# Attention with a relative bias, then a low-rank mixer and a feed-forward block: opening the first feed-forward tiles on three of four channel blocks, an output tile in pieces, and an earlier weight load

## The chip, the cores and the metric

One core of one Trainium2 chip runs the whole program. The metric is device time in microseconds (us), lower is better, from several executions. A profile is one more execution, recorded by the hardware; its span is a microsecond or two shorter than the time of the same run, as the time also contains the launch.

## The reference, cut to what matters

```python
scores = q @ k.T / sqrt(64)              # 8 batches, 8 heads, 576 positions, 64 wide
attn   = softmax(scores + bias[bucket(i - j)])   # bias: 32 buckets, saturates at |i - j| = 128
x      = (attn @ v)                      # heads side by side: 8 x 576 x 512
u      = x + (x.T @ U @ V).T             # mix over positions, rank 32
out    = u + relu(u @ w1) @ w2           # feed-forward: 512 -> 2048 -> 512
```

## The kernel before

The program works on pairs of heads, four to a batch, 32 in all. For each pair TensorE makes the scores, ScalarE their exponentials (`p_sb`), VectorE multiplies the diagonal band by the exponential of the bias (`eb`), TensorE multiplies by the values (`o`), VectorE normalises into `xp`, and TensorE mixes over positions. The bias table goes out to memory once and comes back as overlapping rows, which GpSimd copies in reverse order into `eb`:

```python
def reverse_eb(pr, copy):
    t = ebr.pop(pr)
    ...
        copy(out=eb[:, 2 * pr : 2 * pr + 2, :],
             in_=_ap_with(t, t.offset + 383, [t.ap[0], [384, 2], [-1, 384]]))
```

All matmuls of the feed-forward block are a stream that is cut into the gaps of the attention. `work.run(us)` places as many matmuls as the budget holds, 0.216 us each, in program order:

```python
def chunk(j, tail):                     # one group of 512 tokens; j = 8 is the remainders
    rhs = uT[j % 3] if j < B else uT_rem
    for nt in range(NHT):               # 16 hidden tiles
        gp_ = acc()                     # a 128 x 512 PSUM tile out of three
        for ct in range(4):             # 4 channel blocks, one per pair of heads
            nc.tensor.matmul(gp_, lhsT=w1b[:, ct, ...], rhs=rhs[:, ct, :], ...)
            yield 0.216
        if (nt % 2) if tail else clock["seg"] > 1.5:
            nc.scalar.activation(g[:, nt, :], gp_, AF.Relu)
        else:
            nc.vector.tensor_relu(out=g[:, nt, :], in_=gp_)
    for tt in range(4):                 # 4 output tiles of 128 tokens
        op = acc()
        for nt in range(NHT):
            nc.tensor.matmul(op, lhsT=g[:, nt, ...], rhs=w2b[:, nt, :], ...)
            yield 0.216
        ...                             # add u on VectorE, store
```

The loads that GpSimd issues while batch 0 runs, in program order:

```python
nc.gpsimd.dma_start(out=gate, in_=gp_dram[0:1, 0:2])   # waits until the table is in memory
load_rem(0, 2)                                         # values of batch 0
for t in range(NKT): load_main(0, 2, t)
reverse_eb(0, nc.gpsimd.tensor_copy)
qk0[3] = [first_qk(which, 3) for which in range(2)]
reverse_eb(1, nc.gpsimd.tensor_copy)
load_w1(0)
load_rem(1, 0); load_rem(1, 1)                         # batch 1
qk1 = [[load_pair(which, 0) for which in range(2)]]
def more_loads():
    for pr in (2, 3): load_eb(pr)
    reverse_eb(2, nc.gpsimd.tensor_copy)
    load_w1(1)
    reverse_eb(3, nc.gpsimd.tensor_copy)
    ...
```

And the main loop, three segments to a pair `g`, from the first pair of batch 1 (`g = 4`) on:

```python
for g in range(NPAIR, NG):
    b, pr = divmod(g, NPAIR)
    for seg in range(3):
        ...                             # scores of this segment
        work.run(1.7 if g < 2 * NPAIR + 2 else 2.2)
        ...                             # mixing, transposes, bands, value matmuls
        if seg and NPAIR < g < 2 * NPAIR:
            put_off.pop(0)()            # an addition of batch 0 that was put off
        ...
        if seg == 1 and b > 1 and pr == 1:
            ready[b - 1] = True         # the next group may start
```

The softmax here doesn't subtract the row's maximum and nothing guards it: scores larger than these inputs give would overflow.

## Time and profile before

| | |
|---|---|
| time, median of 3 | 410.99 us (410.21 to 411.16) |
| TensorE idle around the start of the feed-forward work, 36 to 40 us | 1.49 us |
| eb copy of the last pair of batch 0 ends | 31.29 us |
| value matmuls of that pair start | 34.37 us |
| second group of 512 tokens starts | 94.06 us |

In a timeline a line is: start, duration, engine, source line, operation, output<-inputs, shapes, number merged, and in brackets how long the engine was idle before it and what ended that. TensorE ends are modelled, so waits are best read from the distance of two starts, less the 0.216 us (512 columns), 0.055 us (128) or about 0.03 us (65) of a matmul at full clock.

The TensorE timeline where the first group of tokens has ended and the second begins:

```profile
92.66 0.93 PE L601 MATMUL o<-v_bf,p_sb 128*128 128x65 bf16 x25 [0.95 <-DVE xp L626]
93.52 0.61 PE L514 MATMUL sc<-qkT 64*128 64x512 bf16 x4
94.06 1.25 PE L371 MATMUL acc<-uT,w1b 128*128 128x512 bf16 x5
```

The value matmuls wait 0.95 us for the normalisation of the head before them, because their segment has no feed-forward matmuls to hide it.

### The profile page before, as it was taken

How to read it: one execution, taken by the hardware profiler on the slowest of the kernel's cores; microseconds unless marked ns; L12 is line 12 of the kernel's file. 1: busy time of each engine (PE TensorE's matmuls, PEld its weight loads, DVE VectorE, ACT ScalarE, POOL GpSimd, SP SyncE). 2: the span in 40 equal slices, each digit the busy share in tenths (PEclk: the TensorE clock that was granted, in tenths of full speed). 3: DMA queues.
4: the chain of work that ended last, by engine and by line, in shares of the span. 5: the costliest groups of instructions: out<-in, count | busy, mean ns of one | idle time of the engine just before them, and what ended most of it. 6: DMA issues, size and time to landing. Idle time of an engine off the chain costs nothing.

```text
span 408.5 us, 9084 instructions
## 1 busy us (share of the span) xinstructions
PE 389.5 (95%) x3684; PEld 212.8 (52%) x3684; DVE 246.3 (60%) x558; ACT 205.0 (50%) x284; POOL 125.7 (31%) x179
## 2 busy tenths in 40 slices
PE   3779999999999999999999999999999999999995
PEld 1456555555555555555555555555555554444442
DVE  6886897667765667557754785567656732422421
ACT  5877555556655565556555655556555530220310
POOL 3968924454454045404540454040000000000000
PEclk9799999999999999999999999999999999999999
DMA  7999999999999699949996999399022003001013
GB/s 129 170 170 161 114 189 120 118 118 116 174 69 128 131 117 86 129 104 150 92 102 132 128 89 106 94 138 96 14 66 66 14 14 104 26 14 73 18 27 77
DMA packets 162082, 40.68 MB, mean 100 GB/s; under 512 B 151760, under 2 KB 156888, under 8 KB 162040
## 3 DMA queue, kind: packets, MB, share of 16 engines
q0 software_dynamic: 107904, 17.97, 61.2%
q1 hardware_dynamic: 53320, 21.74, 26.2%
q8 instruction: 29, 0.48, 0.5%
q10 hardware_dynamic: 816, 0.39, 0.4%
q14 instruction: 13, 0.11, 0.1%
HBM read 37.84 MB, written 9.45 MB: 116 GB/s over the span
## 4 chain that ended last, share of the span: by engine, by line
PE 82%; DMA 8%; POOL 6%; DVE 2%; issue 1%; ACT 1%; ACTq 0%; DVEq 0%; POOLq 0%
PE acc L386 31%; PE acc L371 28%; PE o L601 10%; PE sc L514 7%; DMA w1b<-in_moe_w_ch_dram 4%; DMA qb<-in_k_dram 3%; PE acc L637 2%; POOL qb L265 2%; POOL v_bf L255 2%; PE acc L653 1%; PE sc L527 1%; PE sc L548 1%; DMA gp_dram<-gp 1%; DVE ob L396 1%; POOL eb L213 1%
## 5 line engine op out<-in xcount | busy, mean ns | idle before, releaser
L523 ACT ACTIVATE p_sb<-sc 128x1024 bf16<-128x1024 f32 x128 | 124.4, 1022 | 100.4 <-PE sc L514 100.3
L386 PE MATMUL acc<-w2b,g 128*128 128x512 bf16 x576 | 132.4, 379 | 0.0
L371 PE MATMUL acc<-uT,w1b 128*128 128x512 bf16 x512 | 119.5, 380 | 0.6 <-DMA w1b<-in_moe_w_ch_dram 0.4
L371 PEld LDWEIGHTS <-w1b 128*128 128x128 bf16 x576 | 53.2, 98 | 72.4 <-issue 13.1
L386 PEld LDWEIGHTS <-g 128*128 128x128 bf16 x576 | 53.6, 98 | 70.6 <-issue 10.6
L382 DVE TENSOR_SCALAR g<-acc 128x512 bf16<-128x512 f32 x95 | 65.3, 690 | 34.4 <-PE acc L371 33.1
L577 DVE TENSOR_TENSOR p_sb<-p_sb,eb 128x768 bf16<-128x768 bf16 (+3 forms) x160 | 71.3, 472 | 10.0 <-ACT p_sb L523 9.4
L601 PEld LDWEIGHTS <-p_sb 128*128 128x128 bf16 x1600 | 56.1, 98 | 9.2 <-DVE p_sb L577 1.6
L601 PE MATMUL o<-v_bf,p_sb 128*128 128x65 bf16 x1500 | 58.0, 194 | 2.3 <-DVE xp L626 0.9
L380 ACT ACTIVATE g<-acc 128x512 bf16<-128x512 f32 x49 | 29.3, 598 | 59.8 <-PE acc L371 44.5
L396 DVE TENSOR_TENSOR ob<-acc,u_tok 128x512 f32<-128x512 f32 x32 | 22.1, 691 | 49.9 <-PE acc L386 49.9
L514 PE MATMUL sc<-qkT 64*128 64x512 bf16 x256 | 41.3, 392 | 1.5 <-ACT qkT L459 0.7
L905 POOL COPY gate<-xp 1x2 bf16<-1x2 bf16 x18 | 3.5, 197 | 121.5 <-DVE xp L626 121.5
L661 DVE TENSOR_TENSOR u_tok<-acc,xp 128x512 bf16<-128x512 f32 x32 | 22.1, 691 | 23.9 <-PE acc L653 23.7
L626 DVE TENSOR_TENSOR xp<-o,rcp 128x320 bf16<-128x320 f32 x60 | 29.5, 492 | 3.2
L255 POOL DMA_DIRECT2D v_bf<-in_v_dram x32 | 28.4, 911 | 1.7 <-DMA w1b<-in_moe_w_ch_dram 1.4
L255 POOL DMA_DIRECT2D qb<-in_k_dram x24 | 21.7, 906 | 5.8 <-DMA w2b<-in_moe_w_ch_dram 4.2
L255 POOL DMA_DIRECT2D qb<-in_q_dram x24 | 21.9, 913 | 4.7 <-DVE g L382 4.7
L557 ACT ACTIVATE p_sb<-sc 128x640 bf16<-128x640 f32 x32 | 22.3, 698 | 0.2
L540 ACT ACTIVATE p_sb<-sc 128x512 bf16<-128x512 f32 x32 | 19.1, 598 | 5.6 <-PE sc L527 3.9
L624 DVE RECIPROCAL rcp<-o 128x5 f32<-128x5 f32 x60 | 11.5, 191 | 13.7 <-PE o L601 13.2
L645 ACT CAST tt<-acc 128x128 bf16<-128x128 f32 x32 | 8.6, 267 | 14.3 <-PE acc L637 13.8
(90 smaller groups left out, 260.8 us busy)
## 6 DMA issues: line engine op xcount, KB each, us to landing
out_dram<-ob SPq DMA_DIRECT2D x32, 256.0 KB, 2.4
v_bf<-in_v_dram POOLq DMA_DIRECT2D x32, 128.0 KB, 5.9
qb<-in_q_dram POOLq DMA_DIRECT2D x27, 128.0 KB, 4.9
qb<-in_k_dram POOLq DMA_DIRECT2D x27, 128.0 KB, 4.9
w1b<-in_moe_w_ch_dram POOLq DMA_DIRECT2D x2, 1024.0 KB, 8.7
w2b<-in_moe_w_ch_dram POOLq DMA_DIRECT2D x2, 1024.0 KB, 12.6
out_dram<-ob SPq DMA_DIRECT2D x8, 128.0 KB, 2.4
stage<-gp_dram SPq DMA_DIRECT2D x4, 192.0 KB, 4.7
```

The costliest lines, as they stand in the source:

```text
L255: nc.gpsimd.dma_start(out=dst, in_=src[b, :, t * 128 : (t + 1) * 128, :].rearrange("h p d -> p h d"),)
L371: nc.tensor.matmul(gp_, lhsT=w1b[:, ct, nt * 128 : (nt + 1) * 128], rhs=rhs[:, ct, :], start=(ct == 0), stop=(ct == 3),)
L380: nc.scalar.activation(g[:, nt, :], gp_, AF.Relu)
L382: nc.vector.tensor_relu(out=g[:, nt, :], in_=gp_)
L386: nc.tensor.matmul(op, lhsT=g[:, nt, tt * 128 : (tt + 1) * 128], rhs=w2b[:, nt, :], start=(nt == 0), stop=(nt == NHT - 1),)
L396: nc.vector.tensor_tensor(out=ob.rearrange("p (a c) -> p a c", a=NPAIR), in0=op.rearrange("p (a c) -> p a c", a=NPAIR), in1=ur, op=ALU.add,)
L514: nc.tensor.matmul(sp[:, hh, :], lhsT=kT[rows, i * 128 : (i + 1) * 128], rhs=qT[rows, 0:S0], start=True, stop=True,)
L523: nc.scalar.activation(P[:, i, :, 0:S0], sp, AF.Exp, scale=scale)
L557: nc.scalar.activation(P4[:, 0:SP], sp.rearrange("p a c -> p (a c)")[:, 0:SP], AF.Exp, scale=scale,)
L577: nc.vector.tensor_tensor(out=t, in0=t, in1=e, op=ALU.mult)
L601: nc.tensor.matmul(o[:, qt * 66 : qt * 66 + 65], lhsT=lhs[:, c0 : c0 + 128], rhs=rhs, start=(kt == NKT and qt == 0), stop=(kt == NKT - 1), ...
L626: nc.vector.tensor_tensor(out=xo[:, :, hh], in0=o[:, :, 0:64], in1=rbc, op=ALU.mult)
```

## The change

The intent: begin the first three hidden tiles on the channel blocks that exist already, so that TensorE has more to do while the last pair of batch 0 is normalised and mixed; move all of w1 and three value loads earlier in GpSimd's order; and shorten what follows the last matmul by storing the last tile in pieces on two queues. The diff, cut:

```diff
     def chunk(j, tail):
+        ahead = [acc() for _ in range(3)] if j == 0 else []
+        for nt, gp_ in enumerate(ahead):
+            for ct in range(3):
+                first_mm(gp_, rhs, nt, ct)
+                yield 0.216
         for nt in range(NHT):
-            gp_ = acc()
-            for ct in range(4):
+            gp_ = ahead[nt] if nt < len(ahead) else acc()
+            for ct in range(3 if nt < len(ahead) else 0, 4):
 ...
         for tt in range(4):
             op = acc()
+            pieces = (0, 256, 384, 512) if j == B and tt == 3 else (0, 512)
+            for c0, c1 in zip(pieces, pieces[1:]):
+                ...                       # 16 matmuls, addition, store of columns c0:c1
+                        (nc.scalar if par else nc.sync).dma_start(...)   # was nc.sync
 ...
     qk0[2] = [first_qk(which, 2) for which in range(2)]
+    load_rem(0, 2)
+    load_main(0, 2, 0)
 ...
     nc.gpsimd.dma_start(out=gate, in_=gp_dram[0:1, 0:2])
-    load_rem(0, 2)
-    for t in range(NKT):
+    for t in range(1, NKT):
         load_main(0, 2, t)
 ...
     load_w1(0)
-    load_rem(1, 0)
-    load_rem(1, 1)
-    qk1 = [[load_pair(which, 0) for which in range(2)]]
+    load_w1(1)
 ...
         reverse_eb(2, nc.gpsimd.tensor_copy)
-        load_w1(1)
+        load_rem(1, 0)
+        load_rem(1, 1)
+        qk1.append([load_pair(which, 0) for which in range(2)])
         reverse_eb(3, nc.gpsimd.tensor_copy)
 ...
     ready[0] = True
-    work.run(0.64)
-    to_copy[1]()
-    mix_t(3, nc.scalar.copy)
-    mix_ut(3, nc.vector.tensor_copy)
+    work.run(0.215 * 9)
+    sc = [ps_s.tile([128, 2, 512], FP32, name="sc")[:, 0, :] for _ in range(2)]
+    mix_t(3, nc.scalar.copy, sc[0])
+    mix_ut(3, nc.vector.tensor_copy, sc[1])
+    work.run(2.2)
+    for copy in fourth_transposes():      # moved here; was ahead of the last pair's values
+        copy()
+    work.run(1.3)
 ...
-            work.run(1.7 if g < 2 * NPAIR + 2 else 2.2)
+            work.run(1.5 if g < 2 * NPAIR + 2 else 2.2)
 ...
-            if seg and NPAIR < g < 2 * NPAIR:
+            if seg and NPAIR <= g < NPAIR + 3:
                 put_off.pop(0)()
```

More of the change, by code (lines that the diff above doesn't have):

```diff
@@ L296 @@
     held = []
+    qk1 = []
     qk2 = ([], [])
@@ L363, with first_mm @@
     clock = {"seg": 0.0}
+    def first_mm(gp_, rhs, nt, ct):
+        nc.tensor.matmul(
+            gp_,
+            lhsT=w1b[:, ct, nt * 128 : (nt + 1) * 128],
+            rhs=rhs[:, ct, :],
+            start=(ct == 0),
+            stop=(ct == 3),
+        )
     def chunk(j, tail):
@@ L367, in chunk @@
         g = gsb.tile([128, NHT, S0], BF16, name="g")
-        for nt in range(NHT):
-            gp_ = acc()
-            for ct in range(4):
-                nc.tensor.matmul(
-                    gp_,
-                    lhsT=w1b[:, ct, nt * 128 : (nt + 1) * 128],
-                    rhs=rhs[:, ct, :],
-                    start=(ct == 0),
-                    stop=(ct == 3),
-                )
+        ahead = [acc() for _ in range(3)] if j == 0 else []
[3 more added lines that the diff above has]
+                yield 0.216
+        for nt in range(NHT):
+            gp_ = ahead[nt] if nt < len(ahead) else acc()
+            for ct in range(3 if nt < len(ahead) else 0, 4):
+                first_mm(gp_, rhs, nt, ct)
                 yield 0.216
@@ L384, in chunk @@
             op = acc()
-            for nt in range(NHT):
-                nc.tensor.matmul(
-                    op,
-                    lhsT=g[:, nt, tt * 128 : (tt + 1) * 128],
-                    rhs=w2b[:, nt, :],
-                    start=(nt == 0),
-                    stop=(nt == NHT - 1),
-                )
-                yield 0.216
             ob = osb.tile([128, DM], FP32, name="ob")
             ur = u_tok[j % 3][:, :, tt, :] if j < B else u_rem[tt]
-            nc.vector.tensor_tensor(
-                out=ob.rearrange("p (a c) -> p a c", a=NPAIR),
-                in0=op.rearrange("p (a c) -> p a c", a=NPAIR),
-                in1=ur,
-                op=ALU.add,
-            )
-            if j < B:
-                nc.sync.dma_start(out=out[j, tt * 128 : (tt + 1) * 128, :], in_=ob)
-            else:
-                for par in range(2):
-                    nc.sync.dma_start(
-                        out=out[2 * tt + par, S0:S, :],
-                        in_=ob[par * 64 : par * 64 + 64, :],
-                    )
+            pieces = (0, 256, 384, 512) if j == B and tt == 3 else (0, 512)
+            for c0, c1 in zip(pieces, pieces[1:]):
+                w = c1 - c0
+                for nt in range(NHT):
+                    nc.tensor.matmul(
+                        op[:, c0:c1],
+                        lhsT=g[:, nt, tt * 128 : (tt + 1) * 128],
+                        rhs=w2b[:, nt, c0:c1],
+                        start=(nt == 0),
+                        stop=(nt == NHT - 1),
+                        skip_group_check=True,
+                    )
+                    yield 0.216 * w / 512
+                nc.vector.tensor_tensor(
+                    out=ob[:, c0:c1].rearrange("p (a c) -> p a c", c=128),
+                    in0=op[:, c0:c1].rearrange("p (a c) -> p a c", c=128),
+                    in1=ur[:, c0 // 128 : c1 // 128, :],
+                    op=ALU.add,
+                )
+                if j < B:
+                    nc.sync.dma_start(out=out[j, tt * 128 : (tt + 1) * 128, :], in_=ob)
+                else:
+                    for par in range(2):
+                        (nc.scalar if par else nc.sync).dma_start(
+                            out=out[2 * tt + par, S0:S, c0:c1],
+                            in_=ob[par * 64 : par * 64 + 64, c0:c1],
+                        )
     ready = [False] * (B + 1)
@@ L500, in fourth_transposes @@
                 nc.tensor.transpose(tp[:, which, t * 128 : (t + 1) * 128], src, ident)
+        copies = nc.scalar.copy, nc.vector.tensor_copy
         return [
-            lambda w=w: nc.scalar.copy(qkT[1][:, 0, w, :], tp[:, w, 0:SP])
-            for w in range(2)
+            lambda w=w: copies[w](qkT[1][:, 0, w, :], tp[:, w, 0:SP]) for w in range(2)
         ]
@@ L630, with mix_t @@
     tt_pr = {}
-    def mix_t(g, eng):
+    def mix_t(g, eng, tp=None):
         b = g // NPAIR
         x = x_pr[g]
-        tp = acc()
+        tp = acc() if tp is None else tp
         for t in range(NT):
@@ L675, in on_pe, with mix_ut @@
         return g < NPAIR
-    def mix_ut(g, copy):
+    def mix_ut(g, copy, tp=None):
         b, pr = divmod(g, NPAIR)
         x, tt = x_pr[g], tt_pr[g]
-        tp = acc()
+        tp = acc() if tp is None else tp
         nc.tensor.matmul(
@@ L862 @@
     kts(3, 3)
-    to_copy = fourth_transposes()
     bands(3, 4, 0, 1)
     normalise(2)
-    to_copy[0]()
     for kt in (4, 0, 1):
```

## The prediction

> **What bounds the kernel now.** I read the page's busy rows first, then the windows by stage, then the TensorE and GpSimd timelines where TensorE is not full, and the timeline of the last microseconds.
>
> ```profile
> PE   3779999999999999999999999999999999999995
> PEclk9799999999999999999999999999999999999999
> 0.00:18.00 18.00, 9.54 (x75) 4.52 (x75) 13.56 (x56) 12.44 (x17) 11.81 (x21) 0.91 0.98 142
> 18.00:36.00 18.00, 15.16 (x278) 11.68 (x277) 15.58 (x37) 13.54 (x20) 13.95 (x20) 0.90 1.29 174
> 36.00:40.00 4.00, 3.00 (x36) 1.77 (x33) 1.97 (x5) 1.99 (x5) 2.57 (x4) 1.00 2.03 157
> 40.00:95.00 55.00, 53.46 (x577) 30.86 (x577) 42.22 (x95) 29.98 (x40) 30.47 (x44) 1.00 1.37 129
> 95.00:325.00 230.00, 230.00 (x2311) 127.26 (x2310) 148.16 (x326) 132.18 (x182) 66.86 (x94) 1.00 0.98 103
> ```
>
> The first two rows are 40 slices of 10.2 us; the others give stretch, length, then busy time of PE, PEld, VectorE, ScalarE, GpSimd. From 95 to 325 us TensorE has no idle time, so nothing there can be gained without fewer matmul columns, and the change removes none. Idle time lies before 95 us, and after the last matmul. The batch 0 to 1 hand-over:
>
> ```profile
> 20.45 0.43 PE L601 MATMUL o<-v_bf,p_sb 128*128 128x65 bf16 x5 [0.62 <-DMA v_bf<-in_v_dram]
> ...
> 36.60 0.59 PE L371 MATMUL acc<-uT,w1b 128*128 128x512 bf16 x2
> 37.56 0.39 PE L371 MATMUL acc<-uT,w1b 128*128 128x512 bf16 x1 [0.36 <-DMA w1b<-in_moe_w_ch_dram]
> 37.78 0.44 PE L637 MATMUL acc<-xp,upad 128*128 128x128 bf16 x5
> 38.58 0.39 PE L681 MATMUL acc<-vpad,tt 128*128 128x512 bf16 x1 [0.36 <-ACT tt L645]
> ...
> 39.98 1.24 PE L371 MATMUL acc<-uT,w1b 128*128 128x512 bf16 x5 [0.29 <-DVE uT L694]
> ```
>
> Matmul ends are modelled, so I work from starts: back-to-back 512-column matmuls start 0.216 us apart, 128-column ones 0.055. Then the three waits are 0.52, 0.52 and 0.45, 1.49 us together; the value-load wait earlier is 0.84 by the same count. GpSimd in that stage:
>
> ```profile
> 27.90 0.75 POOL L265 DMA_DIRECT2D qb<-in_k_dram  x1 [4.05 <-DMA w1b<-in_moe_w_ch_dram]
> 28.63 0.84 POOL L213 COPY eb<-stage 128x768 bf16<-128x768 bf16 x1
> 29.40 0.70 POOL L347 DMA_DIRECT2D w1b<-in_moe_w_ch_dram  x1
> 30.09 1.20 POOL L213 COPY eb<-stage 128x768 bf16<-128x768 bf16 x1
> ```
>
> Here GpSimd itself stops 4.05 us: the 22nd of its DMAs may not be issued before the 14th, the first half of w1, has landed (27.61), because its completion semaphores go round in eight. The eb copy behind it in program order waits too. The end:
>
> ```profile
> 403.71 0.69 DVE L396 TENSOR_TENSOR ob<-acc,u_rem 128x512 f32<-128x512 f32 x1 [2.76 <-PE acc L386]
> 404.43 1.10 SPq L406 DMA_DIRECT2D out_dram<-ob  x2
> ```
>
> After the last matmul come one addition of 0.69, two output DMAs issued one behind the other (the second at 404.94 lands at 407.32), and 1.1 us of closing.
>
> **The Trainium skill.** "DMA: Bandwidth & Descriptors", section "Issuing engines are not separate DMA queues": issuing from several engines saves only sequencer time. In this trace that time is about 0.5 us for the second of two output DMAs. "TensorE: Matmul & The Clock Gate", section "Back-to-back issue gap", gives 81 ns for a sustained 128-column matmul with its weight load and 131 for 512; this trace has 55 and 216, and I use the trace. "SBUF — State Buffer", section "SBUF: two separate sides", says that a GpSimd operation and a VectorE one with two SBUF inputs exclude each other on a shared port pair; the trace agrees: the band multiply of 256 elements takes 314 ns in the mean but 1.32 us at 28.49, beside the eb copy at 28.63.
>
> **The change, part by part.**
>
> (a) Three value loads go ahead of the wait for the small table. The rest then issue about 2.2 us earlier (two of 0.65, one of 0.9). The wait at 20.45 (0.84, and 0.07 just after) goes; from there to 33 us the engines wait on each other, so the shift carries: -0.9.
>
> (b) The second half of w1 is issued right behind the first. Its own wait at 37.56 is hardly worth anything: that matmul also needs the third channel block of uT, whose ScalarE copy ended at 37.39. But the order of GpSimd's DMAs changes: w1 becomes numbers 14 and 15, the loads of batch 1 numbers 16 to 23, and the copy of eb for the last pair stands behind number 23, which must wait for number 15. Landing of number 15: w1's packets started at 20.8, a half takes about 4.95 (20.8 to 27.0 with its tail, landing 27.61). With the queue about a microsecond earlier, two halves end near 31.0 to 31.5. Then 0.28 wake, 0.75 issue, 0.9 copy: the copy ends near 33.0 (32.3 to 33.8) instead of 31.3. VectorE wants it at about 31 (before 32.2, less (a)). Behind it in order are two bands (1.0) and the first half of a normalisation (0.7) before the value matmuls of the last pair can start: 33.0 + 1.75 = 34.75. Without that stall they would start at 34.37 - 0.9 - 0.5 (ten transposes have moved out) = 33.0. So +1.75.
>
> (c) Opening tiles: nine matmuls on blocks 0 to 2 instead of three, then the last pair's two mixing steps back to back on score buffers, then the last blocks. The third matmul still waits for the uT copy: 0.42. The six more hide the normalisation. The step from tt to its matmul still has nothing between: 0.52. The matmul that follows needs the last uT block at once: VectorE copy 0.69 plus 0.26 of hand-over, 0.95, where before the remainder scores lay in between and 0.45 was left. Three evictions then go to ScalarE one after another, and the fourth tile needs the first one's buffer: 0.2 + 0.6, less 0.43 for two other matmuls, 0.4. Sum 2.3 against 1.49: +0.8. The 23 matmuls more that are placed here (26 for 3) are only moved.
>
> (d) Segments of batch 1 get 1.5 us of feed-forward instead of 1.7 (seven matmuls for eight), and the put-off mixing additions start one pair earlier. From 50 to 80 us start-to-start gaps add to 1.6, nearly all released by VectorE. Six evictions (4.1 us of VectorE) are gone from this stage, but its first two pairs now hold four additions of 0.69 that were in the second and third pair. By count VectorE has 17.5 us of work in those two pairs and TensorE 16.5: about the same loss, then relief. +0.3. The stretch near 91.5 (1.1 us idle, a segment with no feed-forward work, as the next tile group opens at the same place) loses about the same, with one such segment more but less VectorE work: 0.
>
> (e) Last tile in pieces of 256, 128, 128: 16 matmuls each at 0.108, 0.055, 0.055 is 3.49 for 3.46. The last addition shrinks from 0.69 to about 0.28 (a 64x128 one takes 0.285): -0.4. The second DMA no longer waits 0.5 for the first: -0.5. A quarter of the bytes in it: about -0.2. Sum -1.1.
>
> Sum: -0.9 + 1.75 + 0.8 + 0.3 - 1.1 = +0.85, or 411.8. I lower it to 411.0: single waits worked out by hand overlap in part, VectorE's bands run free of the eb copies, and budgets as fine as nine matmuls look tuned against a clock.
>
> **Rivals.** One: the queue of GpSimd does bound the early part, as the page's chain has it:
>
> ```profile
> 18.41 9.20 DMA w1b<-in_moe_w_ch_dram
> ...
> 29.40 8.11 DMA w1b<-in_moe_w_ch_dram
> ```
>
> Then getting w1 in eight microseconds earlier would give several microseconds, and the time would be 405 to 408. Against it: TensorE shows only 1.49 us idle between 36 and 40, one third of it released by w1, and the chain reaches these loads only by way of a 12.3 us load that ends in front of transposes at 63.8 which do not read it. Two: the stall in (b) does not happen, as w1 lands by 29.5 or the copy finds its place; then (a) stands and the sum is near 410. Three: the stall in (b) is longer, as w1 shares the engines with the eb loads, and the transposes then wait for batch 1's loads; 413 to 414. Four: VectorE in (d) is relieved at once, most of the 1.6 us goes, and with rival two it is 408.
>
> **Range and chances.** The idle time before 95 us that can be moved is some 3 to 5 us, and the end gives one; no step adds more than 2 to 3. So 411.0, with 407.5 to 414.0 for eight in ten. Two per cent is 8.2 us, more than all of it: faster 0.03, same 0.94, slower 0.03.
>
> **What would show it.** (a) No wait of a value matmul on v_bf near 20 us. (b) A GpSimd wait of some microseconds on w1b at about 27 to 31, an eb copy ending near 33, a VectorE band released by it and TensorE idle 1 to 2 us before the last pair's value matmuls. (c) Feed-forward matmuls released by uT copies for 0.4 and 0.95. (d) Gaps released by VectorE evictions in the first two pairs of batch 1. (e) Last addition near 0.28, last landing about 2.1 us after its issue. If the eb copy comes before 32, (b) is wrong; if the time is under 407, rival one or four has more in it than I give it.

## The result, and the profile after

The changed kernel took 417.03 us (median of 4, 416.49 to 418.27). The ratio to the kernel before is 1.0155, 95% interval 1.0127 to 1.0183. A ratio here is the mean time of one kernel's runs over the mean of the other's of the same rounds, so it is not quite the ratio of the medians. The change costs 6 us; the prediction was no change, with a range of 407.5 to 414.0. Where medians are subtracted below, it is always from the kernel before as it ran on the same chip (410.4 to 411.0).

Line numbers differ: the first feed-forward layer was L371 and is L367, the second L386 and L400, bands L577 and L590, value matmuls L601 and L614. The kernels of the experiments have their own.

The page's busy row and granted clock of the changed kernel, in 40 slices of 10.4 us, and its window from 33.3 to 40 us:

```profile
PE   3776899997999999999999999999999999999995
PEclk9898999999999999999999999999999999999999
33.30:40.00 6.70, 3.37 (x54) 3.08 (x53) 2.95 (x8) 1.83 (x4) 6.17 (x9) 0.76 1.24 79
```

Three slices have fallen: the fourth (31 to 42 us) from 9 to 6, the fifth, with most of the openings, from 9 to 8, and the tenth (94 to 104 us) from 9 to 7. From 33.3 to 40 us TensorE works 3.37 us of 6.70, and its clock was granted at 0.76 in the mean of this execution.

The first dent, in GpSimd's timeline and the one VectorE line that depends on it:

```profile
24.72 1.55 POOL L265 DMA_DIRECT2D qb<-in_q_dram  x2
28.53 0.75 POOL L265 DMA_DIRECT2D qb<-in_k_dram  x1 [2.26 <-DMA w1b<-in_moe_w_ch_dram]
33.84 0.74 POOL L265 DMA_DIRECT2D qb<-in_k_dram  x1 [4.55 <-DMA w1b<-in_moe_w_ch_dram]
34.57 0.84 POOL L213 COPY eb<-stage 128x768 bf16<-128x768 bf16 x1
...
35.44 0.89 DVE L590 TENSOR_TENSOR p_sb<-p_sb,eb 128x512 bf16<-128x512 bf16 x2 [4.68 <-POOL eb L213]
```

GpSimd stands still twice, 2.26 and 4.55 us, each time in front of a load of batch 1 and each time until a half of w1 has landed (28.25 and 33.55). The eb copy behind the second load in program order has had its input since 22.20, and ends at 35.41 instead of 31.29. VectorE waits 4.68 us for it. Then TensorE:

```profile
37.02 1.01 PE L614 MATMUL o<-v_bf,p_sb 128*128 128x65 bf16 x15 [3.33 <-DVE xp L639]
...
41.55 1.67 PE L367 MATMUL acc<-uT,w1b 128*128 128x512 bf16 x7 [0.24 <-ACT uT L707]
43.06 0.44 PE L650 MATMUL sc<-xp,upad 128*128 128x128 bf16 x5
43.86 0.39 PE L694 MATMUL sc<-vpad,tt 128*128 128x512 bf16 x1 [0.36 <-ACT tt L658]
44.09 0.39 PE L699 MATMUL sc<-ident,xp 128*128 128x128 bf16 x4
45.26 0.81 PE L367 MATMUL acc<-uT,w1b 128*128 128x512 bf16 x3 [0.78 <-DVE uT L707]
46.32 1.02 PE L367 MATMUL acc<-uT,w1b 128*128 128x512 bf16 x4 [0.25 <-ACT g L389]
```

The last pair's value matmuls start at 37.02 instead of 34.37: 2.65 us late, after 3.50 us of idle time by the starts. The four waits at the opening tiles are, by starts, 0.41, 0.52, 0.95 and 0.42, together 2.29 us; a fifth of 0.40, at 50.08, waits for the VectorE copy of the transposes that moved.

The second dent, TensorE at the change of groups, to hold against the three lines of before:

```profile
98.82 0.93 PE L614 MATMUL o<-v_bf,p_sb 128*128 128x65 bf16 x25 [0.69 <-DVE xp L639]
99.67 0.61 PE L527 MATMUL sc<-qkT 64*128 64x512 bf16 x4
100.21 0.82 PE L367 MATMUL acc<-uT,w1b 128*128 128x512 bf16 x3
102.66 1.02 PE L367 MATMUL acc<-uT,w1b 128*128 128x512 bf16 x3 [1.62 <-DMA uT<-u_tok]
```

The wait for the normalisation is still there, and a new one has come: three matmuls of the new group run, and the fourth waits (1.79 us by starts) for the last channel block, a transposing DMA issued at 97.49 that lands at 102.61. Before, the same DMA was issued at 91.33, landed at 93.74, and nothing waited. The end:

```profile
410.61 1.05 PE L400 MATMUL acc<-w2b,g 128*128 128x128 bf16 x16 [0.52 <-DVE ob L409]
411.70 0.29 DVE L409 TENSOR_TENSOR ob<-acc,u_rem 128x128 f32<-128x128 f32 x1 [1.14 <-PE acc L400]
412.05 1.05 PE L400 MATMUL acc<-w2b,g 128*128 128x128 bf16 x16 [0.38 <-DVE ob L409]
413.14 0.29 DVE L409 TENSOR_TENSOR ob<-acc,u_rem 128x128 f32<-128x128 f32 x1 [1.14 <-PE acc L400]
```

The additions have become as short as predicted, but the matmuls of the second and third piece wait for the addition of the piece before. From the start of the addition of the tile before last to the end the kernel before takes 8.24 us and this one 8.11.

### The profile page after: what moved, and what is told of

It is laid out like the page before. It is cut to its first block, busy times and chain, and to the rows that moved or that the text cites. A ratio compares the mean times of both kernels' runs of the same rounds, so it can differ in the third digit from the quotient of the medians. Undisturbed runs are those within 1.5% of the kernel's fastest.

```text
span 416.5 us, 9102 instructions
## 1 busy us (share of the span) xinstructions
PE 387.6 (93%) x3656; PEld 215.4 (52%) x3716; DVE 238.7 (57%) x551; ACT 209.9 (50%) x293; POOL 124.7 (30%) x179
## 4 chain that ended last, share of the span: by engine, by line
PE 84%; DMA 7%; DVE 4%; issue 1%; POOL 1%; ACT 1%; SPq 0%; DVEq 0%
PE acc L400 30%; PE acc L367 29%; PE o L614 10%; PE sc L527 7%; DMA w1b<-in_moe_w_ch_dram 3%; PE acc L650 2%; PE acc L666 2%; PE sc L540 1%; PE sc L561 1%; DMA uT<-u_tok 1%; DMA stage<-gp_dram 1%; DVE p_sb L590 1%; DMA tblT<-in_bias_table_dram 1%; DMA gp_dram<-gp 1%; PE acc L501 1%
## 5 line engine op out<-in xcount | busy, mean ns | idle before, releaser
L400 PE MATMUL acc<-w2b,g 128*128 128x512 bf16 (+2 forms) x580 | 129.6, 368 | 2.6 <-DVE ob L409 0.9
L367 PE MATMUL acc<-uT,w1b 128*128 128x512 bf16 x484 | 115.3, 379 | 4.9 <-DMA uT<-u_tok 1.6
L400 PEld LDWEIGHTS <-g 128*128 128x128 bf16 x608 | 55.5, 98 | 70.9 <-issue 12.6
L367 PEld LDWEIGHTS <-w1b 128*128 128x128 bf16 x576 | 53.4, 98 | 73.8 <-issue 15.7
L391 DVE TENSOR_SCALAR g<-acc 128x512 bf16<-128x512 f32 x85 | 58.3, 690 | 38.5 <-PE acc L367 35.5
L590 DVE TENSOR_TENSOR p_sb<-p_sb,eb 128x768 bf16<-128x768 bf16 (+3 forms) x160 | 70.0, 465 | 15.2 <-ACT p_sb L536 9.9
L389 ACT ACTIVATE g<-acc 128x512 bf16<-128x512 f32 x59 | 35.0, 598 | 62.6 <-PE acc L367 62.2
L614 PEld LDWEIGHTS <-p_sb 128*128 128x128 bf16 x1600 | 56.7, 99 | 12.0 <-DVE xp L639 4.5
L614 PE MATMUL o<-v_bf,p_sb 128*128 128x65 bf16 x1500 | 58.4, 194 | 4.8 <-DVE xp L639 4.0
```

The costliest lines, as they stand in the source:

```text
L367: nc.tensor.matmul(gp_, lhsT=w1b[:, ct, nt * 128 : (nt + 1) * 128], rhs=rhs[:, ct, :], start=(ct == 0), stop=(ct == 3),)
L400: nc.tensor.matmul(op[:, c0:c1], lhsT=g[:, nt, tt * 128 : (tt + 1) * 128], rhs=w2b[:, nt, c0:c1], start=(nt == 0), stop=(nt == NHT - 1), s ...
L590: nc.vector.tensor_tensor(out=t, in0=t, in1=e, op=ALU.mult)
L614: nc.tensor.matmul(o[:, qt * 66 : qt * 66 + 65], lhsT=lhs[:, c0 : c0 + 128], rhs=rhs, start=(kt == NKT and qt == 0), stop=(kt == NKT - 1), ...
```

## The experiments

The theory after this reading has three separate losses: the eb copy held up behind a load that waits for w1 (about 3 us), the openings and smaller budgets that leave the change of groups uncovered (about 3 us), and a gain at both ends that is mostly not there. The rivals: the w1 traffic in itself, wherever the eb copy stands; the lower granted clock seen in the profiled execution; and a mere shift, in which the second dent is only an echo of the first.

Twelve kernels ran, all correct. "Of before" and "of after" say which kernel an edit starts from.

### The tail alone

Of before, with only the pieces of the last tile, as in the change's diff (`pieces = (0, 256, 384, 512) ...`, two queues).

> The kernel before with the last output tile in pieces on two queues, and nothing else of the change. In the profile of the changed kernel TensorE waits between the pieces (0.52 and 0.38 us idle by the profile, released by VectorE's addition of the piece before). Theory: the pieces share one PSUM tile, a piece's first matmul waits for the addition that reads the piece before, and this eats the gain: ratio to before 0.998 to 1.001, the two waits in the profile, and about 8.1 us from the start of the addition of the tile before the last to the end, against 8.2 before. Rival (the prediction): the pieces run on without a wait and the end comes 1.1 us earlier, ratio 0.997.

Measured: 409.97 us against 410.53, ratio 0.9988 (0.9975 to 1.0000). The second and third piece wait for VectorE as in the changed kernel; the second of them in the TensorE timeline:

```profile
404.09 1.05 PE L391 MATMUL acc<-w2b,g 128*128 128x128 bf16 x16 [0.38 <-DVE ob L400]
```

### The tail with a PSUM tile for each piece

```diff
         for tt in range(4):
-            op = acc()
             ...
             for c0, c1 in zip(pieces, pieces[1:]):
                 w = c1 - c0
+                op = acc()
```

> As tail_alone, but each piece has a PSUM tile of its own. Theory that the wait comes from the shared PSUM tile: no wait of TensorE between the pieces, and the last 8.2 us shorten by 1.0 to 1.3 us, ratio about 0.997. Rival: small pieces are slow for another reason (weight loads of 128-column matmuls, the landing of the last DMAs): the matmuls of the two small pieces still take over 1.0 us each, and the gain is under 0.4 us.

Measured: 409.29 us against 410.53, ratio 0.9974 (0.9962 to 0.9987). In its timeline of the end the matmuls run through without a wait, and the additions follow 0.9 us apart instead of 1.4:

```profile
404.02 0.29 DVE L400 TENSOR_TENSOR ob<-acc,u_rem 128x128 f32<-128x128 f32 x1 [0.47 <-PE acc L391]
404.91 0.29 DVE L400 TENSOR_TENSOR ob<-acc,u_rem 128x128 f32<-128x128 f32 x1 [0.60 <-PE acc L391]
```

From the addition of the tile before last to the end there are now 6.89 us, against 8.24 before and 8.10 with one tile. So the gain at the end is 1.35 us by these timelines and about 1.2 by the times, and most of it was lost because the three pieces share one tile: with one tile the timelines show 0.14 us, and the times 0.56 with an interval that reaches no change. The Trainium skill, "PSUM — Partial Sum Buffer", section "PSUM bank collisions raise a hardware error", tells to guard PSUM by bank and quadrant, not by address: TensorE may not write one half of a bank while VectorE reads the other. A 128x512 float tile is such a bank, and this trace agrees in so far as the program waits where pieces share the tile (0.52 and 0.38 us in the brackets) and does not where each has its own. Whether the bank asks for this wait, or only the program's bookkeeping of its tiles, no run tells.

### The eb copy ahead of batch 1's loads

Of after:

```diff
         reverse_eb(2, nc.gpsimd.tensor_copy)
+        reverse_eb(3, nc.gpsimd.tensor_copy)
         load_rem(1, 0)
         load_rem(1, 1)
         qk1.append([load_pair(which, 0) for which in range(2)])
-        reverse_eb(3, nc.gpsimd.tensor_copy)
```

> The changed kernel with one edit: the copy of the bias factors of the last pair stands before the loads of batch 1 on GpSimd instead of behind them. Theory that the copy waited behind a load that waits for the second half of w1: the VectorE wait of 4.7 us on this copy is gone, the value matmuls of the last pair start near 34 us instead of 37, and the time falls by 3 to 5 us (the wait, and the lower granted clock after it) to 412 to 414, ratio to before 1.002 to 1.008. Rival: the loads of batch 1 are the bound anyway (they land at 34 to 36.4 us), so that the transposes of batch 1 wait instead and less than 1 us is won.

Measured: 413.74 us against 410.53, ratio 1.0078 (1.0054 to 1.0101). That is 3.2 us over before, where the changed kernel is 6.0 over: 2.8 us back by the medians, 3.2 by the ratios. GpSimd and TensorE:

```profile
21.02 1.91 POOL L213 COPY eb<-stage 128x768 bf16<-128x768 bf16 x2 [0.45 <-DMA stage<-gp_dram]
...
33.95 0.74 POOL L265 DMA_DIRECT2D qb<-in_k_dram  x1 [4.16 <-DMA w1b<-in_moe_w_ch_dram]
...
34.40 0.62 PE L614 MATMUL o<-v_bf,p_sb 128*128 128x65 bf16 x15
```

w1 lands as late as in the changed kernel (33.67), GpSimd still stands 4.16 us, the loads of batch 1 are as late; only the copy is no longer behind them. The value matmuls start at 34.40, as before the change (34.37), without a wait. The cost is neither in the traffic of w1 nor in the late loads: it is the copy's place in the order.

### The same with a budget of 1.3 us

Of the kernel above:

```diff
-            work.run(1.5 if g < 2 * NPAIR + 2 else 2.2)
+            work.run(1.3 if g < 2 * NPAIR + 2 else 2.2)
```

> As eb_ahead, and 1.3 us of feed-forward per segment in batch 1 instead of 1.5, so that the first tile group lasts through the first two segments of the pair in which the next becomes ready. Theory: in the changed kernel those segments are empty, and the next group's fourth matmul waits 1.79 us for the transposing DMA of the last pair; with work left in them the wait goes and the time falls by 1.5 to 2 us against eb_ahead. Rival: the wait is due to that DMA alone (it took 5.1 us to land against 2.4) and remains at whatever place, or the freed segments only move the idle time into pairs 4 to 8: within 0.5 us of eb_ahead.

Measured: 411.13 us against 410.53, ratio 1.0018 (1.0005 to 1.0032); 2.6 us less than the kernel above. TensorE at the change of groups, first with 1.5, then with 1.3:

```profile
97.90 1.02 PE L367 MATMUL acc<-uT,w1b 128*128 128x512 bf16 x3 [0.71 <-DMA uT<-u_tok]
```

```profile
93.28 0.91 PE L614 MATMUL o<-v_bf,p_sb 128*128 128x65 bf16 x25
94.12 0.61 PE L527 MATMUL sc<-qkT 64*128 64x512 bf16 x4
94.66 1.25 PE L367 MATMUL acc<-uT,w1b 128*128 128x512 bf16 x5
```

With 1.3 neither the normalisation nor the transposing DMA is waited for. The count explains it. A group has 128 matmuls, and 17 segments lie between the openings and the point where the next group may start (three for each of pairs 4 to 8, two of pair 9). Before, 125 are left for them at 1.7 / 0.216 = 7.9 a segment: 15.9 segments, one stays empty. The change leaves 102 at 1.5 / 0.216 = 6.9: 14.7 segments, two stay empty. At 1.3 it is 6.0 a segment: 17 segments, none is empty. More put in ahead needs a smaller budget than 1.5, or the stream runs dry at the other end.

The two profiles show where the gain lies: from the first opening matmul to the second group it is 58.34 us instead of 59.49, and from there to the end 314.39 instead of 315.37, together 2.1. The other 0.56 lies before the first opening matmul, where the two programs are the same, so it is scatter.

Why the transposing DMA is late with two empty segments can be read from the issue and landing times of the DMAs around it. Shortly before it GpSimd issues three loads for batch 2:

| | first of three loads issued | third landed | transposing DMA issued | landed |
|---|---|---|---|---|
| before | 85.63 | 91.72 | 91.33 | 93.74 |
| after | 93.91 | 102.45 | 97.49 | 102.61 |
| openings alone (below) | 90.63 | 98.37 | 94.22 | 98.61 |
| eb copy ahead, 1.5 | 90.06 | 97.67 | 93.65 | 97.86 |
| eb copy ahead, 1.3 | 86.85 | 94.05 | 90.94 | not recorded |

Where two segments are empty the attention comes to this DMA 3.6 us after the loads, instead of 5.7 before and 4.1 with 1.3. The loads are then still under way, and in all three such kernels the DMA lands 0.16 to 0.24 us behind the last of them. That it is held up by their packets is what this pattern suggests; no run took these loads away.

### The openings alone

Of after, with the value loads, the load order and the tail put back as before; what stays are the openings, the moved transposes, the budget of 1.5 and the put-off additions.

> The kernel before with the opening tiles, the mixing on score buffers and the budgets of the change alone: value loads, order of the weights and last tile as before. Theory: these parts alone lose time: the four waits of the opening (0.4, 0.5, 0.95, 0.4) against 1.5 us before, and 1 to 2 us where the second tile group waits for the transposing DMA: ratio 1.005 to 1.009 (2 to 3.5 us). Rival: nearly all of the 6 us came from the GpSimd stall; this kernel is within 1 us of before, ratio 0.998 to 1.0025.

Measured: 413.84 us against 410.72, ratio 1.0081 (1.0067 to 1.0095). The waits at the change of groups in TensorE's timeline:

```profile
95.54 0.93 PE L610 MATMUL o<-v_bf,p_sb 128*128 128x65 bf16 x25 [0.69 <-DVE xp L635]
...
98.65 1.02 PE L367 MATMUL acc<-uT,w1b 128*128 128x512 bf16 x3 [0.89 <-DMA uT<-u_tok]
```

The loss of 3.1 us and both waits are there with the load order of before, where nothing stalls at 33 us: the second dent is not an echo of the first. The second group's first matmul starts at 96.94 here, at 94.06 before. The value matmuls of the last pair start at 34.73, 0.36 later than before. This profiled execution is 4.1 us longer than that of before (it is the longest of its four): 2.5 of them come between these two points, and 1.2 after the second, where the DMA is waited for.

### The load order put back

Of after, with w1's second half and the loads of batch 1 in the old order; value loads, openings and tail stay.

```diff
     load_w1(0)
-    load_w1(1)
+    load_rem(1, 0)
+    load_rem(1, 1)
+    qk1.append([load_pair(which, 0) for which in range(2)])
 ...
         reverse_eb(2, nc.gpsimd.tensor_copy)
-        load_rem(1, 0)
-        load_rem(1, 1)
-        qk1.append([load_pair(which, 0) for which in range(2)])
+        load_w1(1)
         reverse_eb(3, nc.gpsimd.tensor_copy)
```

> The changed kernel with one part undone: the second half of w1 and the loads of batch 1 are issued in the order of the kernel before. Theory: this removes the GpSimd stall as eb_ahead does, and having w1 early is itself worth only what its wait adds to the wait for the uT copy, 0.3 us (0.70 against 0.41 in the profiles of open_alone and eb_ahead): 413.7 to 414.3, ratio to before 1.007 to 1.010. Rival: with nine opening matmuls the early w1 is what makes them possible, and without it a microsecond or more is lost: over 414.8, ratio over 1.0105.

Measured: 413.98 us against 410.55, ratio 1.0078 (1.0054 to 1.0102): the same as with the eb copy ahead. The stall of GpSimd is then the one of before:

```profile
28.49 0.74 POOL L265 DMA_DIRECT2D qb<-in_k_dram  x1 [4.01 <-DMA w1b<-in_moe_w_ch_dram]
```

The value matmuls start at 34.20, and the early w1 is not worth anything that can be seen: without it TensorE waits 0.86 us for w1 at 38.05, where 0.24 of waiting for the uT copy stand otherwise, and the time is the same within 0.3 us. Two ways of taking the stall away give back the same 2.6 to 2.8 us.

### The value loads alone

Of before:

```diff
     qk0[2] = [first_qk(which, 2) for which in range(2)]
+    load_rem(0, 2)
+    load_main(0, 2, 0)
 ...
     nc.gpsimd.dma_start(out=gate, in_=gp_dram[0:1, 0:2])
-    load_rem(0, 2)
-    for t in range(NKT):
+    for t in range(1, NKT):
         load_main(0, 2, t)
```

> The kernel before with the three value loads ahead of the wait for the small table, and nothing else. In all runs with this part the table is written 0.55 us later (6.63 to 6.71 against 6.07 to 6.10) and the eb loads land 1.2 to 2 us later. Theory: what the values gain the table loses; the value matmuls of the first pair end at about the same time as before (21.2 to 21.5), ratio 0.998 to 1.002. Rival (the prediction): the wait goes and 0.9 us are won, ratio 0.998 or less, with the first pair's value matmuls ending near 20.6.

Measured: 410.97 us against 410.72, ratio 1.0010 (0.9994 to 1.0027): no gain. In the profiled run the wait for the values is gone and the first pair's value matmuls are through 1.0 us earlier (the last starts at 20.47 instead of 21.46), but most of this is not the loads' doing. Between 15 and 20 us TensorE's clock was granted at 0.50 in the profile of the kernel before, and at 1.00 here. It was 1.00 too in the profile of the tail alone, which is the same program as before up to its last tile, and there the last of these matmuls starts at 20.61, with the waits for values (0.30 and 0.27 us in the brackets). So at the same clock the loads gain 0.14 us: a wait of 0.72 us for the band product, in the brackets at 18.78, has taken the place of the waits for values. Six runs lie in two groups, 409.6 to 409.8 and 410.9 to 411.8.

One cost of the three loads could be read. They are issued by GpSimd at 5 to 7 us, just where VectorE builds the bias table with 15 small casts. The groups of these casts, in the kernel before and in the changed one (min/median/max in ns):

```profile
L180 DVE CAST gp<-gmT x15: 152/155/165, 4.8 to 5.9; 8x6 bf16<-8x6 f32 x4, 8x12 bf16<-8x12 f32 x2, 8x8 bf16<-8x8 f32 x1, 8x10 bf16<-8x10 f32 x1
```

```profile
L180 DVE CAST gp<-gmT x15: 153/293/655, 5.2 to 6.3; 8x6 bf16<-8x6 f32 x4, 8x12 bf16<-8x12 f32 x2, 8x8 bf16<-8x8 f32 x1, 8x10 bf16<-8x10 f32 x1
```

And in the kernel with the eb copy ahead, the last casts beside a load's issue in the timeline:

```profile
5.74 0.86 DVE L180 CAST gp<-gmT 8x26 bf16<-8x26 f32 x3
...
5.64 0.96 POOL L255 DMA_DIRECT2D v_bf<-in_v_dram  x1
```

The last of these casts takes 0.70 us instead of 0.15 to 0.17 and ends at 6.61 us; the issue ends at 6.60. The Trainium skill, "SBUF — State Buffer", section "SBUF: two separate sides", calls the port pair that VectorE and GpSimd share an exclusive lock, taken for a whole instruction. The trace agrees in part: the two end within 0.01 us, but the casts of 5.66, 5.74 and 5.83, which also start after the issue, take the usual 0.16. In all profiles with this load early the casts that start by 5.88 are not held up, and those from 5.91 on are. In the changed kernel the table goes out at 6.71 us instead of 6.07, the eb rows for the first two pairs land at 16.42 and 18.27 instead of 14.66 and 16.05, and w1, behind the eb copies in GpSimd's order, is issued at 19.40 instead of 18.41. Alone, the profiled run of this experiment had the table out at 6.06, so the cast won the race there, and the rows still landed at 15.38 and 17.14, later than before. The loads brought forward compete with the rows they were moved ahead of. Why the runs form two groups stays open; that the race for the port decides it was only argued, and the variant below that has the table on time again gained nothing.

### The openings in another order

Of the kernel with 1.3: the nine matmuls by channel block instead of by tile, three of them between the two mixing steps, and the transposes between mixing and the last blocks.

```diff
-        for nt, gp_ in enumerate(ahead):
-            for ct in range(3):
+        for ct in range(3):
+            for nt, gp_ in enumerate(ahead):
 ...
-    work.run(0.215 * 9)
-    sc = [ps_s.tile([128, 2, 512], FP32, name="sc")[:, 0, :] for _ in range(2)]
-    mix_t(3, nc.scalar.copy, sc[0])
-    mix_ut(3, nc.vector.tensor_copy, sc[1])
-    work.run(2.2)
+    work.run(0.215 * 6)
+    sc = ps_s.tile([128, 2, 512], FP32, name="sc")
+    mix_t(3, nc.scalar.copy, sc[:, 0, :])
+    work.run(0.215 * 3)
+    mix_ut(3, nc.vector.tensor_copy, sc[:, 1, :])
     for copy in fourth_transposes():
         copy()
-    work.run(1.3)
+    work.run(3.5)
```

> eb_ahead_13 with another order of the same work at the hand-over: the nine opening matmuls go block by block instead of tile by tile, three of them stand between the two mixing steps of the last pair, and the transposes of batch 1 stand right behind the second step. Theory: the waits of 0.41, 0.52 and 0.95 us are a matter of order; they go, or shrink to 0.4 in the last case, and 1.3 to 1.9 us are won against eb_ahead_13: about 409.4, ratio 0.997. Rival: VectorE in the first pairs of batch 1 is the bound, and what TensorE wins here it waits there: within 0.6 us of eb_ahead_13, ratio over 1.0.

Measured: 410.38 us (six runs, two of them at 411.69 and 413.78) against 410.72, ratio 1.0015 (0.9989 to 1.0040). The interval covers both a gain and a loss, so the time alone decides nothing. Against the kernel with 1.3 it is 0.9 us by the medians and 0.1 by the ratios, less than the 1.3 to 1.9 of the theory. The profile shows the two waits that were aimed at:

```profile
39.70 0.38 PE L694 MATMUL sc<-vpad,tt 128*128 128x512 bf16 x1
...
41.15 0.81 PE L367 MATMUL acc<-uT,w1b 128*128 128x512 bf16 x3 [0.29 <-DVE uT L707]
```

The wait for tt (0.52) is gone and the one for the last uT block has shrunk from 0.95 to 0.46; the waits that are left are 0.62, 0.46 and 0.41 by starts, 1.49 us, which is exactly the figure before the change. In waits, the opening gained nothing over the kernel before even so.

### The same with a PSUM tile for each piece

Of the kernel above, with `op = acc()` inside the loop over the pieces.

> fill_order, and each piece of the last tile in a PSUM tile of its own. If the two gains add up, 0.7 to 1.2 us less than fill_order: 408.3 to 408.7, ratio to before 0.994 to 0.995, faster than both kernels. If the last microseconds are set by the landing of DMAs, no difference to fill_order beyond 0.3 us.

Measured: 409.25 us against 410.72, ratio 0.9971 (0.9958 to 0.9983). That is 1.1 under the kernel above, as expected, though not the 408.3 to 408.7 that was put down. The scatter of the last kernel is not seen here. It is the first that holds all parts of the change and beats the kernel before.

### Only the remainder's value loads ahead; none ahead; more evictions on ScalarE

Three variants ran together. Of the last kernel, with only the two remainder loads ahead:

```diff
     load_rem(0, 2)
-    load_main(0, 2, 0)
 ...
-    for t in range(1, NKT):
+    for t in range(NKT):
         load_main(0, 2, t)
```

> fill_own, with only the two small value loads ahead of the wait for the table and the third one behind it again. In the profiles with all three ahead the last cast that builds the table takes about 0.70 us instead of 0.165, from 5.91 to 6.61, and ends with the GpSimd load issued at 5.64 (0.96 us). Theory: that issue and the cast exclude each other[...], and the cast loses the race by some 40 ns in most executions. Without the third load there the last cast takes 0.17 us, the table is written near 6.1 instead of 6.65, and 0.3 to 0.9 us are won against fill_own: 408.4 to 408.9, ratio 0.994 to 0.996. Rival: the table lands late because the early loads crowd the DMA queues; then it stays near 6.6 and nothing is won.

Measured: 410.01 us against 410.44, ratio 0.9979 (0.9960 to 0.9997). The 408.4 to 408.9 of the theory is missed. The table goes out at 6.08 us, as before, so the port race at the casts is at most a small part of what the early loads cost. The eb rows still land late (15.38 and 17.17), and the wait for the values has come back, longer than before the change, in TensorE's timeline:

```profile
21.69 0.44 PE L614 MATMUL o<-v_bf,p_sb 128*128 128x65 bf16 x5 [1.25 <-DMA v_bf<-in_v_dram]
```

Of the kernel with own tiles again, with all value loads back where they were before the change:

```diff
-    load_rem(0, 2)
-    load_main(0, 2, 0)
 ...
     nc.gpsimd.dma_start(out=gate, in_=gp_dram[0:1, 0:2])
-    for t in range(1, NKT):
+    load_rem(0, 2)
+    for t in range(NKT):
         load_main(0, 2, t)
```

> fill_own with all value loads back behind the wait. Theory: table at 6.1 as before, but the wait of the first pair's value matmuls (0.84 us) comes back: within 0.4 us of fill_own, ratio 0.996 to 0.998. Rival: early value loads are worth their 0.9 us: this one is 0.5 to 1 us slower than best_rem.

Measured: 408.09 us against 410.44, ratio 0.9933 (0.9916 to 0.9950). It is the fastest of all, 2.3 us under the kernel before and 8.9 under the changed one, and faster than either expectation. Its busy row has neither dent:

```profile
PE   3789999999999999999999999999999999999996
```

The eb rows land at 14.45 and 15.68, and the second group starts at 93.51. Against the variant with two loads ahead it gains 1.9 us, and the six runs of the one do not overlap the six of the other: here the early value loads do harm. By the profiles the two differ only before the first feed-forward matmul (36.16 against 38.39 us; from there to the end both take 370.52). Part of that is the granted clock, which between 20 and 25 us was 0.67 here and 0.50 there, and between 15 and 20 us 0.98 and 0.50; its share in the 1.9 us was not separated.

Last, of the variant with the remainder loads ahead, more of the first group's evictions on ScalarE:

```diff
-            if (nt % 2) if tail else clock["seg"] > 1.5:
+            if (nt % 2) if tail else clock["seg"] > (0.8 if j == 0 else 1.5):
```

> best_rem, and in the first tile group evictions go to ScalarE once 0.8 us of feed-forward are done in a segment instead of 1.5. Theory: the gaps left in pairs 4 to 6 (0.29, 0.43, 0.40, 0.32, 0.34 us in the profile of fill_own, released by VectorE evictions) are VectorE's share; half the evictions on ScalarE remove over half of these 1.8 us: 0.6 to 1.2 us less than best_rem. Rival: ScalarE's evictions delay the exponentials, and the gaps come back in front of the value matmuls: within 0.4 us of best_rem, or slower.

Measured: 410.95 us, ratio 1.0006 (0.9983 to 1.0029), 0.9 above its own base by the medians, with intervals that overlap. No relief is seen, and ScalarE's evictions now hold TensorE up, as at 51 us in its timeline:

```profile
51.35 0.38 PE L501 MATMUL acc<-ident,qb 128*128 128x128 bf16 x4 [0.74 <-ACT g L389]
```

### The sum

| part | measured by | us |
|---|---|---|
| openings, budgets and moved additions | openings alone | +3.1 |
| eb copy behind the stalled load | after, less the same with the copy ahead | +2.8 |
| value loads | alone | +0.25 (interval covers 0) |
| tail | alone | -0.56 |
| together | | 5.6 |
| the whole change | | 6.0 |

The remaining 0.4 us is within the scatter of the runs. The lower granted clock from 33.3 to 40 us in the profiled execution (its 418.27 us is the longest of four) explains part of that one execution: its value matmuls start 55 ns apart for a while, where they start about 30 ns apart elsewhere, and from the first of them to the first opening matmul it takes 3.70 us instead of 2.23. The other three runs, at 416.49 to 417.44, have a mean clock of 0.996 against 0.991 and are still 5.5 to 6.5 us above before. So the clock is not the cause of the loss.

## Why the prediction was wrong, point by point

**Step (b), +1.75, was right in mechanism and too small.** GpSimd waits for w1 in front of the last load before the eb copy, and the copy waits with it: all as written. The failed term is the landing of w1's second half, put at 31.0 to 31.5; it was 33.55. The estimate had the queue start "about a microsecond earlier", on the strength of (a). In fact w1 was issued a microsecond later (19.40 against 18.41), behind a table and eb rows that were late. The first half then landed at 28.25, where 27.61 less a microsecond was supposed, and the second 5.30 behind it instead of the 4.95 that the step gives for a half (its own figures, 20.8 to 27.0, make 6.2). The early value loads are not the whole reason: in the fastest kernel, which has none of them, w1 is issued at 18.17 and its second half still lands at 33.02, so 1.23 us of earlier issue are worth 0.53 of landing. What else holds w1 up was not found. From there on the chain held: 0.29 to wake, 0.74 to issue, 0.84 to copy, then 1.61 from the copy's end to the value matmuls (1.75 predicted). They start at 37.02 instead of the 34.75 put down. The cost was 2.8 us. Rival three, the longer stall with 413 to 414, was nearest; whether w1 shares the engines with the eb loads, as it says, was not tested.

**Step (d), +0.3 and "0" at the stretch near 91.5, was the second error.** The +0.3 was too small: over pairs 4 to 8 the gaps by starts that another engine ended add to about 2.2 us, against 1.6 before. At the stretch near 91.5 the step saw that one more segment would be without feed-forward work, and then called it even because VectorE had less to do there. What it left out is that the next group, which starts in the segment after, needs a transposing DMA, and that DMA doesn't become faster when the segments become shorter. It runs into three loads that are still under way and takes 4.2 to 5.1 us instead of 2.4, and the group's fourth matmul waits, 1.79 us in the changed kernel and 1.05 with the openings alone. With the other waits of the under-filled stretch the budget of 1.5 costs 2.6 us by the medians and 2.1 by the profiles, as the run with 1.3 shows: 1.0 of it after the second group has started, where the DMA is waited for, and 1.15 before. A finer separation was not made. The division of matmuls by segments, done above in three lines, would have shown two empty segments in advance.

**Step (c), +0.8, was right in its waits.** Of the four waits, 0.42, 0.52, 0.95 and 0.4 were predicted and 0.41, 0.52, 0.95 and 0.42 measured. Missing was one of 0.40 for the copy of the moved transposes. Where the order of work was fixed, starts and known durations gave the waits to hundredths. What they cost in time was not measured apart from the budgets.

**Step (a), -0.9, failed.** The wait for the values fell only from 0.84 to 0.66 us in the changed kernel, since the loads still behind the gate came later (the gate's own issue moved from 9.89 to 10.82). By itself the change puts a wait for the bands in the place of the wait for the values, moves the value matmuls forward by 0.14 us at the same clock, and gives +0.25 in time, with an interval around zero. The step treated GpSimd's issues as free for VectorE, and the early loads as free for the eb rows. Neither is.

**Step (e), -1.1, failed for the most part.** The terms were right, but they suppose that TensorE goes on while VectorE adds. With one PSUM tile the program makes it wait: -0.56 by the times, whose interval reaches zero, and -0.14 by the timelines. With a tile per piece it is -1.24 and -1.35, so the sum of the terms was about right for a program that the change did not contain.

**Rivals one, two and four.** Nothing of several microseconds came from w1's early arrival (the load order put back loses nothing), so rival one is out. The stall did happen, so is rival two. A relief of VectorE in the first pairs of batch 1 is not seen: the gaps over pairs 4 to 8 grew, as said under (d).

**The sum.** The lowering from 411.8 to 411.0, for overlap and for what looked like tuned budgets, went the wrong way. The terms that failed were all on one side: most supposed that work moved forward finds its engines and queues free.

## What to carry to other kernels

When a load is moved up in an engine's order, list what stands behind it in that order and what the queue's completion semaphores make it wait for; a small copy that needs none of it should go ahead of the loads. When work is placed ahead of a loop that is filled by a budget, work out again how many rounds the rest will fill, as a stream that ends early is paid for at the next group's first dependency. Pieces of one tile that go through two engines in turn needed separate PSUM tiles here, or the second engine's part was only put in series with the first's. And before a shift in a profile is put down to an edit, look at the granted clock of the same stretch in both: of the 1.0 us that the early value loads seemed to gain at 20 us, all but 0.14 came with the clock.

## What the Trainium skill lacked or had wrong

- "SBUF — State Buffer", section "SBUF: two separate sides", describes the trap in one direction, a VectorE operation that keeps GpSimd from writing descriptors. The runs show what looks like the other one: a cast of 8x32 elements on VectorE took 0.70 us instead of 0.15 to 0.17 beside a GpSimd load's issue of 0.96, and they ended at 6.61 and 6.60. The general rule of the lock covers it, but the example and the size are lacking, and so is that casts which started in the first 0.2 us of the issue were not held up.
- "TensorE: Matmul & The Clock Gate", section "Back-to-back issue gap", gives 81 and 131 ns for sustained matmuls of 128 and 512 columns with their weight loads. In a stream of such pairs this case measures 55 and 216 ns, which is what the same section calls the gap of a single matmul.
- No page that I read says how many DMAs GpSimd may have under way before an issue must wait. In this program the completion semaphores of its DMAs go round in eight, so the 22nd and 23rd waited for the 14th and 15th to land: 2.26 and 4.55 us of standing still.
- No page that I read has the time of a small transposing DMA from issue to landing in a loaded program. The one for a pair's 128x512 block took 2.4 us in the kernel before and 5.1 us in the changed one, at the same place in the program, and landed 0.16 us behind three loads issued ahead of it by another engine.
